# Buffers placed by the planner, a second tuning of its order, and eight planned weight chunks in an attention and two-layer feed-forward kernel

## The chip, the cores and the metric

The kernel runs on one core of one Trainium2 chip. The metric is device time in microseconds (us) of one execution, the median of several; lower is better. TensorE is PE in the rows, its weight loads PEld, VectorE DVE, ScalarE ACT, GpSimd POOL, and SyncE, which issues the DMAs, SP.

## What is computed

Per batch (2) and head (8), with 768 positions of width 64: queries and keys are hashed by the signs of six projections, a score counts only where the two hashes agree, and softmax times `v` follows. The result is the input (1536 tokens, width 512) of two feed-forward layers (512 to 2048 to 512), the first with a leaky rectifier, the second with `h*cos(h)`.

```python
mask = q_bucket[:, :, :, None] == k_bucket[:, :, None, :]
scores = scale * np.matmul(q, k.transpose(0, 1, 3, 2))
scores = np.where(mask, scores, -1000000000.0)
scores = scores - np.max(scores, axis=-1, keepdims=True)
attn = np.exp(scores)
attn = attn / (np.sum(attn, axis=-1, keepdims=True) + 1e-09)
x = np.matmul(attn, v)             # then, per layer:
h = x @ w_in
g = np.maximum(0.01 * h, h)        # layer 1; h * np.cos(h) in layer 2
x = g @ w_out
```

## The kernel before, in words

Every float32 operand of a matmul is split into a rounded part ("hi") and a remainder ("lo"), and three products stand for one.

**Attention.** 16 heads `n`, each in six key blocks `k`. Per head and block the items are: `mm` (2 matmuls, L284), a product whose row maximum `mr` (DVE, L290) gives the row's shift; `qk` (4 matmuls, L361 and L362), the scores; `ex` and `cv` (ACT), exponential and its rounded copy; `sub` (L383), the remainder; `pv` (4 matmuls) and `pw` (2 matmuls), both L396, values times hi and lo. Once a head: `bm` and `bw` (hash bits, L268 and L274), `rt` and `fl` (the maxima turned into a row), `pe`, `ev`, then `lc`, `rc`, `dw`, `rr`, `xm`, `xh`, `xl`, which divide by the sum and split the result into `XH` and `XL`. A head has 80 matmuls of 384 columns and one small one.

`sub` has two kinds, chosen by a letter per block in `LO`. With G, ACT writes the exponential to a tile `pf` in SBUF (L371), copies it rounded (L379), and POOL subtracts. With V, ACT computes the exponential twice, once rounded into `ph` (L368), once in place in PSUM (L376), and DVE subtracts from PSUM; the PSUM tile is taken until that is done. `mm`, `qk`, `bm`, `rt` and the sums of `v` share three PSUM tiles `st`.

**Feed-forward.** A step `s` is one block of 128 hidden columns `f` by 512 tokens: `mi` (12 matmuls, L655), `ga`, `gm`, `gh`, `gl` (activation and its split), `mo` (12 matmuls into four accumulators `y`, L700); after four blocks `ye` takes `y` away (L709, L711). Steps 0 to 11 use weight chunks 0 to 3 three times, steps 12 to 15 chunks 4 to 7. A chunk (1 MB of float64) is loaded (`wload`) and converted in seven pieces: `w0` (ACT, L580), `w1` and `w2` (DVE, L581 and L582), `w3` and `w4` (DVE, L583 and L573), `w5` (ACT, L584), `w6` (POOL, L577). `w3` and `w4` read two SBUF tensors.

**What sets the order.** `Plan.order` (L112) is a list scheduler: items with costs (`COST`), priorities (`KEY`, `FIX`, `CHUNK_KEY`) and dependencies are placed one after the other on five queues, and the order so found is the program order of each engine. It covers the attention, feed-forward steps 0 to 11 and the first `CHUNKS` = 6 chunks. Tiles come from pools that hand out their buffers in turn; the plan waits for the use that lies a ring's length back. From step 12 on `Moe.rest` (L745) writes the program: per step `Feed.tick` (L598) emits one stage of a chunk in work, and `Feed.until` (L617) emits the rest of a chunk at the step that needs it.

Of the kernel before, what the change touches and what calls it, by code (L numbers as in the profile page):

```python
# [28 lines left out]
TB = 512  # L29
NR = 4  # L30
LO = [{0: 'GGGGGG', 1: 'VGVGVV', 2: 'GVGGVG', 12: 'GGGVGV', 13: 'GVGGGG', 14: 'VGVVGV', 15: 'GGVGVV'}.get(n, "VGGGVG") for n in range(NH)]
CHUNKS = 6
# [3 lines left out]
    load=-118, hi=-28, d2=-23, d3=18, lo=-83, dl=-28, bm=-14.2, bw=-32, db2=-57, db1=-38, mm=-8.1, mr=-25,  # L36
    rt=-10, fl=82, neg=-50, dr=-48, de=-28, qk=0.8, ex=-6, cv=-29, sub=-21, pe=86, pv=4.7, pw=3.2, ev=-15,
    lc=10, rc=27, dw=-3, rr=-17, xm=56, xh=57, xl=20, vload=5, vh=25, vl=1, sv=-10.3, sh=101, sl=26, wload=58,
    w0=45, w1=73, w2=10, w3=62, w4=-37, w5=99, w6=-57, mi=-5, ga=-8, gm=-40, gh=80, gl=-47, mo=56, ye=2,
)  # L40
FIX = {
# [7 lines left out]
}  # L49
CHUNK_KEY = (95.9, 69.7, 115.6, 142.2, 66.7, 109.6, 173.8, 129.6)  # L50
# [43 lines left out]
class Plan:  # L94
# [4 lines left out]
    def __init__(self, rings, free):  # L99
        self.rings, self.free = rings, dict(free)  # L100
        self.items, self.index = [], {}

    def add(self, name, e, kind, key, fn, after=(), take=None, give=(), cost=None, moe=False):
        deps = [self.index[d] for d in after if d is not None and d in self.index]
        it = dict(name=name, e=e, kind=kind, key=(key, len(self.items)), fn=fn, deps=deps, take=take, give=list(give),
                  cost=COST[kind] if cost is None else cost, out=[], left=len(deps), moe=moe, before=[])
        for d in deps:
            d["out"].append(it)
        self.items.append(it)
        self.index[name] = it  # L110

    def order(self):  # L112
        free = {e: self.free.get(e, 0.0) for e in "PVAGQ"}
        ready = {e: [] for e in "PVAGQ"}
        taken = {r: [] for r in self.rings}
# [7 lines left out]
        def start(it):  # L123
            t = max(free[it["e"]], it["at"])
            r = it["take"]
            if r is not None:
                n = len(taken[r]) - self.rings[r]
                if n >= 0:
                    t = max(t, taken[r][n].get("end", 1e9))
            return t  # L130

        while len(done) < len(self.items):
# [26 lines left out]
            if it["take"] is not None:  # L159
                it["slot"] = {}  # L160
                taken[it["take"]].append(it["slot"])
                n = len(taken[it["take"]]) - 1 - self.rings[it["take"]]
                it["before"] = [taken[it["take"]][n]["by"]] if n >= 0 else []
            for g in it["give"]:
                self.index[g]["slot"].update(end=end + 0.06, by=it)
# [10 lines left out]
def attention(tc, ctx, plan, xp, dr_p, XH, XL, AT, VH, VL, YX, qkt, v, proj, cst, fd, more_raws, heads=NH):  # L176
# [3 lines left out]
    if True:  # L180
        pool = lambda n, b, **kw: ctx.enter_context(tc.tile_pool(name=n, bufs=b, **kw))
        con = pool("con", 1)
        raw_p = pool("raw", 2)
        vraw_p = pool("vraw", 1)
        phi_p = pool("phi", 3)
        plo_p = pool("plo", 3)
        pf_p = pool("pf", 2)
        sm_p = pool("sm", 3)
        sv_p = pool("svp", 1)
        st_ps = pool("st", 3, space=bass.MemoryType.PSUM)  # L190
        pv_ps = pool("pvp", 1, space=bass.MemoryType.PSUM)
# [9 lines left out]
        raw = {0: raw_p.tile([128, S], F32, name="raw")}  # L201
# [5 lines left out]
        E = [con.tile([128, S], F32R, name=f"e{i}") for i in range(2)]  # L207
        SV = [con.tile([128, 4, 128], F32R, name=f"sv{i}") for i in range(2)]
# [12 lines left out]
        neg = con.tile([1, S], F32, name="neg")  # L221
        G.memset(neg, -1.0)
        ident = con.tile([128, 128], F32R, name="ident")
# [21 lines left out]
        def load_qk(n):  # L245
            raw[n] = raw_p.tile([128, S], F32, name="raw")
# [33 lines left out]
        def max_mm(n, t):  # L280
            at = AT[n % NR]
            ps = st_ps.tile([128, 2, 512], F32, name="st")
# [31 lines left out]
        def load_v(g):  # L314
            vraw[g] = vraw_p.tile([128, C, 4, 64], F32, name="vraw")
# [12 lines left out]
        def sum_v(g):  # L328
            ps = st_ps.tile([128, 2, 512], F32, name="st")
# [25 lines left out]
        def qk(n, k):  # L355
            at = AT[n % NR]
            ps = st_ps.tile([128, 2, 512], F32, name="st")
# [43 lines left out]
        drs = {}  # L401
# [67 lines left out]
        for n in range(heads):  # L469
# [4 lines left out]
            if n:  # L474
                do("load", n, "Q", load_qk, n, take="raw" if n > 1 else None, after=[("load", n - 1), ("dr", n - 3)])
# [3 lines left out]
                do("lo", n, "G", lo, n, after=[("hi", n)], give=[("load", n)] if n > 1 else ())  # L479
# [379 lines left out]
```

## Time and profile before

| | us |
|---|---|
| median of 3 runs | 821.01 (820.14 to 821.43) |
| the profiled execution | 821.24 |
| its span, first to last instruction | 819.4 |
| PE busy in it | 786.8 |
| DVE, ACT, POOL busy | 479.5, 438.4, 432.4 |

The profile lists, for one execution, the busy time of each engine, and for each instruction what ended the engine's idle time before it. The program is in order on each engine, so a wait holds up all that stands behind it. Attention takes the span up to 264.8 us, where the first `mi` begins; feed-forward steps follow until the end. Busy shares are averages over stages; what a wait costs is read in its stage.

### The profile page before, as it was taken

What the parts mean: (1) busy time and instruction counts of PE and PEld (TensorE: products, weight loads), DVE (VectorE), ACT (ScalarE), POOL (GpSimd) and SP (SyncE); (2) the same over time, 40 slices, a digit from 0 to 9 for tenths busy, and PEclk for the clock granted to TensorE, in tenths of its full rate; (3) what the DMA queues carried; (4) which work ended last, traced back from release to release, by engine and by line L of the source; (5) the groups of instructions that cost most, each with busy time, mean ns of one, the idle gap of its engine ahead of it and who ended that gap; (6) DMA issues with size and microseconds to landing.
All of it is one profiled execution on the core that took longest, in us unless ns stands there. A gap on an engine that the chain in (4) does not pass through costs nothing. (4 is left out here: it accounts for less than half of the span.)

```text
span 819.4 us, 9862 instructions
## 1 busy us (share of the span) xinstructions
PE 786.8 (96%) x3648; PEld 667.8 (81%) x3648; DVE 479.5 (59%) x579; ACT 438.4 (53%) x630; POOL 432.4 (53%) x282
## 2 busy tenths in 40 slices
PE   6999999999899999779999999999999999999998
PEld 4899999989799788558888888887788888888886
DVE  7666666656777952337666356456747737743333
ACT  3777878867789424224333224355656555544442
POOL 8768887977778512223455334846623533532221
PEclk9999999999999999889999999999999999999999
DMA  6534534524531610112222112102202210000012
GB/s 177 149 84 111 147 91 102 138 64 109 167 110 57 215 68 1 52 52 90 70 98 103 52 52 102 52 4 100 102 1 66 89 52 1 0 1 2 0 52 103
DMA packets 24264, 63.19 MB, mean 77 GB/s; under 512 B 7684, under 2 KB 11428, under 8 KB 20120
## 3 DMA queue, kind: packets, MB, share of 16 engines
q1 hardware_dynamic: 24216, 62.56, 25.1%
q8 instruction: 29, 0.48, 0.2%
q14 instruction: 19, 0.16, 0.1%
HBM read 46.21 MB, written 3.19 MB: 60 GB/s over the span
## 5 line engine op out<-in xcount | busy, mean ns | idle before, releaser
L687 POOL TENSOR_TENSOR gl<-gf,gh 128x512 fp32r<-128x512 f32 x88 | 123.1, 1399 | 298.8 <-ACT gh L681 238.0
L700 PE MATMUL y<-gh,at 128*128 128x512 f32 x576 | 181.0, 395 | 1.6 <-ACT ys L709 1.6
L655 PE MATMUL h<-XH,at 128*128 128x512 f32 x576 | 143.9, 391 | 0.0
L383 POOL TENSOR_TENSOR pl<-pf,ph 128x768 fp32r<-128x768 f32 x62 | 116.3, 1884 | 40.1 <-ACT ph L379 33.3
L700 PEld LDWEIGHTS y<-gh,at 128*128 128x128 f32 x576 | 107.6, 187 | 28.1 <-ACT ys L709 2.0
L655 PEld LDWEIGHTS h<-XH,at 128*128 128x128 f32 x576 | 108.0, 188 | 24.9 <-POOL at L577 0.5
L290 DVE TENSOR_REDUCE mx<-st 128x1 fp32r<-128x768 f32 x96 | 90.9, 956 | 43.4 <-PE st L284 41.4
L700 PE MATMUL y<-gl,at 128*128 128x512 f32 x288 | 113.6, 395 | 0.7 <-POOL gl L687 0.7
L662 ACT ACTIVATE gf<-h 128x512 f32<-128x512 f32 x48 | 28.7, 598 | 143.1 <-PE h L655 127.0
L672 DVE TENSOR_TENSOR gf<-h,gf 128x512 f32<-128x512 f32 x48 | 33.1, 690 | 108.7 <-ACT gf L662 108.6
L666 ACT ACTIVATE ki<-h 128x512 int32<-128x512 f32 x48 | 28.7, 598 | 107.1 <-PE h L655 107.1
L655 PE MATMUL h<-XL,at 128*128 128x512 f32 x288 | 77.0, 389 | 0.0
L667 DVE SCALAR_TENSOR_TENSOR gf<-ki,h 128x512 f32<-128x512 int32 x48 | 33.0, 687 | 72.9 <-ACT ki L666 66.9
L361 PE MATMUL st<-at 77*128 77x384 f32 x192 | 67.4, 351 | 3.8 <-DVE mx L290 2.3
L700 PEld LDWEIGHTS y<-gl,at 128*128 128x128 f32 x288 | 53.9, 187 | 14.3 <-POOL gl L687 1.1
L362 PE MATMUL st<-at 128*128 128x384 f32 x192 | 65.2, 340 | 0.0
L577 POOL TENSOR_TENSOR at<-wsc,at 128x1024 fp32r<-128x1024 f32 x24 | 60.3, 2512 | 7.1 <-ACT at L584 7.1
L655 PE MATMUL h<-XH,wx 128*128 128x512 f32 x192 | 52.6, 417 | 11.2 <-ACT wx L584 10.5
L655 PEld LDWEIGHTS h<-XL,at 128*128 128x128 f32 x288 | 54.1, 188 | 11.4
L681 ACT ACTIVATE gh<-gf 128x512 fp32r<-128x512 f32 x96 | 59.8, 623 | 4.0 <-DVE gf L672 2.3
L371 ACT ACTIVATE pf<-st 128x768 f32<-128x768 f32 x62 | 50.1, 808 | 19.3 <-PE st L362 17.6
L676 DVE SCALAR_TENSOR_TENSOR gf<-gf,h 128x512 f32<-128x512 f32 x48 | 32.9, 685 | 46.2 <-ACT gf L675 46.2
(95 smaller groups left out, 1467.1 us busy)
## 6 DMA issues: line engine op xcount, KB each, us to landing
wrvh<-in_w_dram SPq DMA_DIRECT2D x16, 1024.0 KB
wrvl<-in_w_dram SPq DMA_DIRECT2D x16, 1024.0 KB
at<-at SPq DMA_DIRECT2D x63, 192.0 KB
raw<-in_qk_dram SPq DMA_DIRECT2D x15, 384.0 KB
vraw<-in_v_dram SPq DMA_DIRECT2D x4, 768.0 KB
yx<-dr SPq DMA_DIRECT2D x16, 192.0 KB
out_dram<-ys SPq DMA_DIRECT2D x6, 256.0 KB
out_dram<-yx SPq DMA_DIRECT2D x6, 256.0 KB
```

Source lines behind the costliest of these rows:

```text
L290: V.reduce_max(mx[n][:, t:t + 1], mps.pop((n, t))[:, :, 0:HS], axis=AX.XY)
L361: T.matmul(o, at[0:R76 + 1, 2, kc], at[0:R76 + 1, 0, COL[h]], start=True, stop=False)
L362: T.matmul(o, at[:, 3, kc], at[:, 1, COL[h]], start=False, stop=True)
L371: A.activation(pf[n, k], sps.pop((n, k)), AF.Exp, scale=SCALE)
L383: (V if LO[n][k] == "V" else G).tensor_tensor(halves(plo[n, k]), pf.pop((n, k)), halves(f32(phi[n, k])), op=ALU.subtract)
L577: G.tensor_tensor(lf, sc, f32(hf), op=ALU.subtract)
L655: self.tc.nc.tensor.matmul(ps, w[:, 0, k], x[:, k, cols], start=(j == 0), stop=(j == 3 * KT - 1))
L667: nc.vector.scalar_tensor_tensor(g, ki, -TWOPI, ps, op0=ALU.mult, op1=ALU.add)
L672: nc.vector.tensor_tensor(g, ps, g, op=ALU.max)
L681: self.tc.nc.scalar.activation(gh, self.gs[s], AF.Copy)
L687: (nc.vector if s < GLV else nc.gpsimd).tensor_tensor(gl, g, f32(gh), op=ALU.subtract)
L700: self.tc.nc.tensor.matmul(y, w[:, 1, e], x, start=(j == 0 and i == 0), stop=(j == GRP - 1 and i == 2))
```

## The change

`Plan` keeps for each ring the time at which each of its buffers comes free and gives an item the one that is free first; `plan.tile` hands the tile out by that place, and the pools are gone. 131 of the 229 times that `st` is taken, the buffer is not the next in turn; `phi` and `plo` also leave the turn, the other rings keep it. `LO`, `KEY`, `FIX`, `CHUNK_KEY` and six costs have new numbers: `w3` and `w4` from 0.95 to 1.15, `w5` 0.93 to 1.06, `w6` 2.37 to 2.4, `fl` 0.45 to 0.55, `ga` 0.63 to 0.6. By `LO`, 53 of the 96 `sub` are on DVE instead of 34; in heads 3 to 10 it is four of six instead of two. `CHUNKS` is 8. Tiles of a few bytes are allocated behind the large ones, so that large tiles start at multiples of 64 bytes.

```diff
-LO = [{0: 'GGGGGG', 1: 'VGVGVV', 2: 'GVGGVG', 12: 'GGGVGV', 13: 'GVGGGG', 14: 'VGVVGV', 15: 'GGVGVV'}.get(n, "VGGGVG") for n in range(NH)]
-CHUNKS = 6
+LO = [{0: 'GGGVGG', 1: 'VGGGVG', 2: 'GGVGVG', 11: 'GGGVGV', 12: 'GGVVGV', 13: 'GVGGGG', 14: 'VGVVVV', 15: 'VGVVVV'}.get(n, "VGVGVV") for n in range(NH)]
+CHUNKS = 8
-CHUNK_KEY = (95.9, 69.7, 115.6, 142.2, 66.7, 109.6, 173.8, 129.6)
+CHUNK_KEY = (132.0, 106.0, 116.9, 111.2, 249.3, 102.4, 235.2, 115.5)
...
+    def tile(self, ring):
+        return self.tiles[ring][self.place]
...
-            r = it["take"]
-            if r is not None:
-                n = len(taken[r]) - self.rings[r]
-                if n >= 0:
-                    t = max(t, taken[r][n].get("end", 1e9))
+            if it["take"] is not None:
+                t = max(t, min(end for end, _ in places[it["take"]]))
...
+                ring = places[it["take"]]
+                j = it["place"] = min(range(len(ring)), key=lambda j: ring[j][0])
+                it["before"] = [ring[j][1]] if ring[j][1] else []
+                ring[j] = (1e9, None)
             for g in it["give"]:
-                self.index[g]["slot"].update(end=end + 0.06, by=it)
+                g = self.index[g]
+                places[g["take"]][g["place"]] = (end + 0.06, it)
...
-            ps = st_ps.tile([128, 2, 512], F32, name="st")
+            ps = plan.tile("st")
...
-        neg = con.tile([1, S], F32, name="neg")
+        neg = con.tile([C, 128], F32, name="neg")
...
-            do("wload", c, "Q", wload, c, key=key - 8, after=[("pw", 11, C - 1), ("wload", c - 1), ("w4", c - 2)])
+            do("wload", c, "Q", wload, c, key=key - 8, after=[("pw", 11 if c < 6 else NH - 1, C - 1), ("wload", c - 1), ("w4", c - (2 if c < 6 else 4))])
...
-        ps = self.h[s] = self.h_ps.tile([128, TB], F32, name="h")
+        ps = self.h[s] = self.HP[s % 4]
...
-        sc_p = ctx.enter_context(tc.tile_pool(name="wscp", bufs=2))
+        sc_p = ctx.enter_context(tc.tile_pool(name="wscp", bufs=1))
+        sums = xp.tile([128, 64], F32, name="sums")
```

Three places on DVE show how the order moves. In the order of the change a name carries the number of its buffer, and its lines are those of the changed kernel: L299 is `mr`, L392 `sub`, L283 `bw`, L419 `rc`, L681 `gm`, L695 `gl`, L717 `ye`, and L589, L590, L591, L581 are `w1` to `w4`.

First, between steps 5 and 9 of the first layer. Before, from the sixth `gm` on:

```order
L687 TENSOR_TENSOR gl<-gf,gh 128x512
L672 TENSOR_TENSOR gf<-h,gf 128x512 x2
L687 TENSOR_TENSOR gl<-gf,gh 128x512
L672 TENSOR_TENSOR gf<-h,gf 128x512
L711 TENSOR_SCALAR ys_2902<-y_2976 128x512
L711 TENSOR_SCALAR ys_2904<-y_2978 128x512
L687 TENSOR_TENSOR gl<-gf,gh 128x512
```

Now, where `wsc_77` with `wrvh_2309` is chunk 6 and `wsc_78` with `wrvl_2310` chunk 7:

```order
L589 TENSOR_SCALAR wsc_77<-wsc_77 128x1024
L681 TENSOR_TENSOR gf_2327<-h_2341,gf_2327 128x512
L590 TENSOR_SCALAR wsc_77<-wsc_77 128x1024
L589 TENSOR_SCALAR wsc_78<-wsc_78 128x1024
L681 TENSOR_TENSOR gf_2326<-h_2338,gf_2326 128x512
L590 TENSOR_SCALAR wsc_78<-wsc_78 128x1024
L591 SCALAR_TENSOR_TENSOR wsc_78<-wrvl_2310,wsc_78 128x1024
L581 SCALAR_TENSOR_TENSOR wsc_78<-wrvl_2310,wsc_78 128x1024
L591 SCALAR_TENSOR_TENSOR wsc_77<-wrvh_2309,wsc_77 128x1024
L581 SCALAR_TENSOR_TENSOR wsc_77<-wrvh_2309,wsc_77 128x1024
L717 TENSOR_SCALAR ys_2347<-y_2343 128x512
L717 TENSOR_SCALAR ys_2349<-y_2345 128x512
```

The eight DVE pieces of chunks 6 and 7 now stand ahead of the `ye` of step 3; before, they stood behind the `gm` of steps 13 and 14.

Second, chunks 0 and 1 among heads 12 to 14. Before:

```order
L383 TENSOR_TENSOR pl<-st,ph 128x768
L581 TENSOR_SCALAR wsc<-wsc 128x1024
L582 TENSOR_SCALAR wsc<-wsc 128x1024
L274 TENSOR_SCALAR at_70<-st,cs 44x768
L583 SCALAR_TENSOR_TENSOR wsc<-wrvh_2332,wsc 128x1024
L573 SCALAR_TENSOR_TENSOR wsc<-wrvh_2332,wsc 128x1024
L290 TENSOR_REDUCE mx<-st 128x1 x2
```

Now:

```order
L589 TENSOR_SCALAR wsc_77<-wsc_77 128x1024
L283 TENSOR_SCALAR at_71<-st_109,cs 44x768
L392 TENSOR_TENSOR plo_93<-st_110,phi_90 128x768
L590 TENSOR_SCALAR wsc_77<-wsc_77 128x1024
L392 TENSOR_TENSOR plo_92<-st_108,phi_89 128x768
L299 TENSOR_REDUCE mx_107<-st_110 128x1
L299 TENSOR_REDUCE mx_107<-st_108 128x1
L589 TENSOR_SCALAR wsc_78<-wsc_78 128x1024
L590 TENSOR_SCALAR wsc_78<-wsc_78 128x1024
L299 TENSOR_REDUCE mx_107<-st_108 128x1
L591 SCALAR_TENSOR_TENSOR wsc_78<-wrvl_1887,wsc_78 128x1024
L392 TENSOR_TENSOR plo_92<-st_109,phi_88 128x768
```

`w3` and `w4` of chunk 0 no longer stand between `bw` of head 15 and the `mr` of head 14; they come after the last `mr` of head 15, and those of chunk 1 stand singly.

Third, the end of attention, from the last `sub` of head 14. Before:

```order
L581 TENSOR_SCALAR wsc<-wsc 128x1024
L582 TENSOR_SCALAR wsc<-wsc 128x1024
L583 SCALAR_TENSOR_TENSOR wsc<-wrvh_2332,wsc 128x1024
L383 TENSOR_TENSOR pl<-st,ph 128x768
L573 SCALAR_TENSOR_TENSOR wsc<-wrvh_2332,wsc 128x1024
L383 TENSOR_TENSOR pl<-st,ph 128x768
L411 RECIPROCAL rc<-lc 128x6
L383 TENSOR_TENSOR pl<-st,ph 128x768
```

Now:

```order
L590 TENSOR_SCALAR wsc_77<-wsc_77 128x1024
L591 SCALAR_TENSOR_TENSOR wsc_77<-wrvh_1886,wsc_77 128x1024
L581 SCALAR_TENSOR_TENSOR wsc_77<-wrvh_1886,wsc_77 128x1024
L392 TENSOR_TENSOR plo_92<-st_109,phi_90 128x768
L392 TENSOR_TENSOR plo_91<-st_110,phi_89 128x768
L589 TENSOR_SCALAR wsc_78<-wsc_78 128x1024
L590 TENSOR_SCALAR wsc_78<-wsc_78 128x1024
L392 TENSOR_TENSOR plo_92<-st_108,phi_90 128x768
L419 RECIPROCAL sums<-sums 128x6
L591 SCALAR_TENSOR_TENSOR wsc_78<-wrvl_1887,wsc_78 128x1024
L392 TENSOR_TENSOR plo_93<-st_109,phi_88 128x768
L392 TENSOR_TENSOR plo_91<-st_110,phi_89 128x768
```

Head 15 has five `sub` on DVE instead of three, and seven pieces of chunks 2 and 3 among them instead of four.

## Rows read from the trace of the kernel before

**Rows 1.** The profile's first part: busy us, share of the span, instructions.

```profile
PE 786.8 (96%) x3648; PEld 667.8 (81%) x3648; DVE 479.5 (59%) x579; ACT 438.4 (53%) x630; POOL 432.4 (53%) x282
```

**Rows 2.** Windows of PE, steps 12 to 15: us, PE busy (x), granted clock, DMA, GB/s.

```profile
323.10:328.64 5.54, 5.54 (x26) 1.00 0.00 0
328.64:361.43 32.79, 21.55 (x74) 0.79 0.19 64
```

**Rows 3.** Timeline of PE, steps 14 and 15: start, us, engine line op [idle <-releaser].

```profile
339.06 2.07 PE L655 MATMUL h<-XH,wx 128*128 128x512 f32 x4 [4.71 <-ACT wx L584]
...
353.38 2.07 PE L655 MATMUL h<-XH,wx 128*128 128x512 f32 x4 [5.79 <-ACT wx L584]
```

**Rows 4.** Timeline of DVE, 307 to 338 us: start, us, then as in rows 3.

```profile
307.90 0.69 DVE L711 TENSOR_SCALAR ys<-y 128x512 f32<-128x512 f32 x1 [7.75 <-PE y L700]
...
332.88 1.79 DVE L581 TENSOR_SCALAR wsc<-wsc 128x1024 f32<-128x1024 f32 x1
334.70 0.69 DVE L582 TENSOR_SCALAR wsc<-wsc 128x1024 int32<-128x1024 int32 x1
335.43 1.23 DVE L583 SCALAR_TENSOR_TENSOR wsc<-wrvh,wsc 128x1024 int32<-128x1024 int32 x1
336.69 1.22 DVE L573 SCALAR_TENSOR_TENSOR wsc<-wrvh,wsc 128x1024 int32<-128x1024 int32 x1
```

**Rows 5.** Windows: us, PE, PEld, DVE, ACT, POOL busy (x), granted clock, DMA, GB/s.

```profile
163.95:170.42 6.47, 4.72 (x18) 4.21 (x18) 2.93 (x6) 2.22 (x3) 4.34 (x3) 0.74 0.20 40
215.10:232.50 17.40, 14.18 (x69) 13.33 (x69) 16.24 (x18) 11.79 (x15) 8.08 (x4) 0.90 0.61 187
262.20:264.90 2.70, 2.17 (x13) 1.77 (x12) 2.59 (x5) 2.70 (x4) 1.88 (x1) 1.00 0.47 112
```

**Rows 6.** The same view, the even stretch of attention.

```profile
100.00:160.00 60.00, 60.00 (x342) 57.76 (x341) 38.30 (x50) 47.64 (x63) 51.53 (x29) 1.00 0.44 108
```

**Rows 7.** Timelines of PE, ACT and POOL at 163 to 167 us.

```profile
166.21 0.71 PE L284 MATMUL st<-at 76*128 76x384 f32 x2 [1.75 <-ACT pf L371]
...
165.35 0.81 ACT L371 ACTIVATE pf<-st 128x768 f32<-128x768 f32 x1 [0.83 <-POOL pl L383]
...
163.48 3.60 POOL L383 TENSOR_TENSOR pl<-pf,ph 128x768 fp32r<-128x768 f32 x2
```

**Rows 8.** Timelines of PE and DVE at 220 to 225 us.

```profile
224.15 0.44 PE L361 MATMUL st<-at 77*128 77x384 f32 x1 [2.30 <-DVE mx L290]
...
220.36 2.75 DVE L573 SCALAR_TENSOR_TENSOR wsc<-wrvh,wsc 128x1024 int32<-128x1024 int32 x1
```

**Rows 9.** Groups by line and form, 20 to 210 us: busy us, mean ns.

```profile
L290 DVE TENSOR_REDUCE mx<-st 128x1 fp32r<-128x768 f32 x77 | 73.5, 958 | 37.4 <-PE st L284 35.5
L383 DVE TENSOR_TENSOR pl<-st,ph 128x768 fp32r<-128x768 f32 x24 | 23.0, 958 | 11.6 <-ACT st L376 10.6 <-POOL pl L383 0.4 <-POOL XL L432 0.3
L274 DVE TENSOR_SCALAR at<-st,cs 44x768 fp32r<-44x768 f32 x13 | 14.1, 1086 | 12.7 <-PE st L268 6.0 <-POOL yx L423 2.6 <-issue 1.7
...
L383 POOL TENSOR_TENSOR pl<-pf,ph 128x768 fp32r<-128x768 f32 x50 | 91.8, 1843 | 33.5 <-ACT ph L379 27.9 <-DMA raw<-in_qk_dram 1.9 <-PE st L284 1.7
L432 POOL TENSOR_TENSOR XL<-yx,XH 128x768 fp32r<-128x768 f32 x5 | 9.2, 1841 | 0.0
...
L376 ACT ACTIVATE st<-st 128x768 f32<-128x768 f32 x24 | 19.3, 806 | 0.0
```

**Rows 10.** The same groups, whole span: `gl` on DVE.

```profile
L687 DVE TENSOR_TENSOR gl<-gf,gh 128x512 fp32r<-128x512 f32 x8 | 11.6, 1465 | 1.0 <-ACT gh L681 1.0
```

**Rows 11.** Timeline of DVE and POOL at 270 to 313 us.

```profile
270.85 0.68 DVE L687 TENSOR_TENSOR gl<-gf,gh 128x512 fp32r<-128x512 f32 x1
...
312.57 1.29 POOL L687 TENSOR_TENSOR gl<-gf,gh 128x512 fp32r<-128x512 f32 x1 [16.40 <-ACT gh L681]
```

**Rows 12.** Timelines of POOL and ACT at the start.

```profile
11.89 1.82 POOL L254 TENSOR_TENSOR at<-raw,at 128x768 fp32r<-128x768 f32 x1
...
7.51 0.84 ACT L250 ACTIVATE at<-raw 128x768 fp32r<-128x768 f32 x1 [0.95 <-DMA raw<-in_qk_dram]
```

More of the change, by code (lines that the diff above doesn't have):

```diff
@@ L105, in add @@
         it = dict(name=name, e=e, kind=kind, key=(key, len(self.items)), fn=fn, deps=deps, take=take, give=list(give),
-                  cost=COST[kind] if cost is None else cost, out=[], left=len(deps), moe=moe, before=[])
+                  cost=COST[kind] if cost is None else cost, out=[], left=len(deps), moe=moe, before=[], place=0)
         for d in deps:
@@ L114, in order @@
         ready = {e: [] for e in "PVAGQ"}
-        taken = {r: [] for r in self.rings}
+        places = {r: [(0.0, None)] * k for r, k in self.rings.items()}
         wire = port = 0.0
@@ L173, in order, with attention @@
         return done
-def attention(tc, ctx, plan, xp, dr_p, XH, XL, AT, VH, VL, YX, qkt, v, proj, cst, fd, more_raws, heads=NH):
+def attention(tc, ctx, plan, sums, dr_p, XH, XL, AT, VH, VL, YX, qkt, v, proj, cst, fd, more_raws, heads=NH):
     nc = tc.nc
@@ L182, in attention, with ring @@
         con = pool("con", 1)
[L183 to L191, printed above, removed]
+        psum = pool("psum", 1, space=bass.MemoryType.PSUM)
+        def ring(name, shape, dtype=F32, p=con):
+            plan.tiles[name] = [p.tile(shape, dtype, name=f"{name}{i}") for i in range(plan.rings[name])]
+        ring("raw", [128, S])
+        ring("vraw", [128, C, 4, 64])
+        ring("phi", [128, S], F32R)
+        ring("plo", [128, S], F32R)
+        ring("pf", [128, S])
+        E = [con.tile([128, S], F32R, name=f"e{i}") for i in range(2)]
+        SV = [con.tile([128, 4, 128], F32R, name=f"sv{i}") for i in range(2)]
+        ring("svt", [128, 2, 2, 64], F32R)
+        ring("mt", [C, 2, 128])
+        ident = con.tile([128, 128], F32R, name="ident")
+        ring("mx", [128, C], F32R)
+        ring("st", [128, 2, 512], p=psum)
+        ring("pv", [128, 2, 512], p=psum)
+        DR = [dr_p.tile([1, S], F32, name=f"dr{i}") for i in range(4)]
         OS = [YX[:, i * S:(i + 1) * S] for i in range(2)]
         RR, XX = (YX[:, i * S:(i + 1) * S] for i in (2, 3))
-        LC, RC = (xp.tile([128, 4, C], F32, name=n) for n in ("lc", "rc"))
+        LC, RC = (sums[:, i * 4 * C:(i + 1) * 4 * C].rearrange("p (a b) -> p a b", b=C) for i in range(2))
         cs = con.tile([128, 130], F32, name="cs")
@@ L200, in attention @@
         Q.dma_start(pj[64:128], proj)
-        raw = {0: raw_p.tile([128, S], F32, name="raw")}
+        raw = {0: plan.tiles["raw"][0]}
         COL = [slice(h * HS, (h + 1) * HS) for h in range(2)]
@@ L281, in max_mm @@
             at = AT[n % NR]
-            ps = st_ps.tile([128, 2, 512], F32, name="st")
+            ps = plan.tile("st")
             for h in range(2):
@@ L328, in sum_v @@
         def sum_v(g):
[L329 removed]
+            ps = plan.tile("st")
             vs = (VH[g % 2], VL[g % 2])
@@ L474, in attention @@
             if n:
-                do("load", n, "Q", load_qk, n, take="raw" if n > 1 else None, after=[("load", n - 1), ("dr", n - 3)])
+                do("load", n, "Q", load_qk, n, take="raw", after=[("hi0", 0), ("load", n - 1), ("dr", n - 3)])
                 do("hi", n, "A", hi, n, after=[("load", n)] + old)
@@ L678, in high @@
     def high(self, s):
-        gh = self.g_p.tile([128, TB], F32R, name="gh")
-        gl = self.g_p.tile([128, TB], F32R, name="gl")
+        gh, gl = (t[s % (LAG + 1)] for t in (self.GH, self.GL))
         self.tc.nc.scalar.activation(gh, self.gs[s], AF.Copy)
@@ L694, in mm_out @@
         j = f % GRP
-        if j == 0:
-            self.ys[l, b] = [self.y_ps.tile([128, TB], F32, name=f"y{e}") for e in range(KT)]
         for e in range(KT):
-            y = self.ys[l, b][e]
+            y = self.YP[e]
             for i, (w, x) in enumerate(((wh, gh), (wl, gh), (wh, gl))):
@@ L808, in emit @@
                 seen.add(id(it))
+                plan.place = it["place"]
                 it["fn"]()
```

118 lines of the change are left out of this document (55 added, 63 removed), and 15 rows, old and new, of the table FIX.

## The prediction

> **What bounds the kernel now.** I read the busy times first. PE is busy 786.8 us, 96% of the span, and no other engine above 59% [rows 1], so the time falls only where PE waits or runs slowly. The next view is therefore PE stage by stage, in windows. The reader is to see three kinds of place. The dearest is steps 13 to 15 of the first layer: step 12 takes 5.54 us, and the next 32.79 us hold only three steps, at a granted clock of 0.79 [rows 2]. The timeline of PE names the releaser: steps 14 and 15 wait 4.71 and 5.79 us for the conversion of chunks 6 and 7 on ACT [rows 3]. Behind ACT stands DVE: chunk 6's four DVE pieces follow each other only from 332.88 us on [rows 4], because the unplanned feeder gives out one stage per step. The other two kinds lie in attention, one stretch at 164 us and one at 215 to 232 us, with the granted clock at 0.74 and 0.90 [rows 5]. The even stretch between them is full: 342 matmuls in 60.00 us, 0.175 us each [rows 6]. That pace is the yardstick for the two bad stretches.
>
> **The change, part by part.** All sums are against the profiled execution of 821.24 us, 0.2 above the median of 821.01.
>
> *Chunks 6 and 7 are planned.* Three steps at 5.54 us would take 16.6 us; they take 32.79 [rows 2]. If both chunks are ready, 16.2 us go, the stretch at half clock behind each wait included. No instruction is added: the same seven pieces a chunk move ahead, past `gm` and `ye` on DVE and past some `ga` on ACT, and their two loads go ahead of and behind the last `rr` on SP. What covers them? A chunk's DVE pieces cost 0.69, 0.69, 1.23 and 1.22 [rows 4] (the first took 1.79 there, beside a POOL subtraction; I set it as the second), 3.8 us, so 7.7 us for two. They now stand around `gm` of steps 7 and 8 and ahead of `ye` of step 3, where DVE sat idle for 7.75 us [rows 4], while PE has eight `mi` in a row. They fit, barely. If that cover fails, `ye` comes late and the next `mo`, which wants its accumulators, waits. Upwards the price is bounded by stretching: one such piece took 2.75 us beside POOL [rows 8] instead of 1.22, 1.5 more, and two of the last four stand beside POOL's `w6` of the other chunk, 3.1 us. A wait of 1.75 us cost 3.3 in all (next term), so up to 5.8. I take nothing, since POOL has a gap of 16.40 us there [rows 11]; the term lies between 10.4 and 16.2.
>
> *Two of six `sub` per head leave POOL for DVE in heads 3 to 10.* At 164 us PE waits 1.75 us for a `st` tile that ACT empties, ACT waits for a `pf` tile, and POOL is two `sub` behind [rows 7]. The stretch holds 18 matmuls, worth 3.2 us, and lasts 6.47 [rows 5]: 3.3 us. With two `sub` of 1.84 us less [rows 9] POOL is relieved of 3.7 us a head, more than that wait. I take 3.3, down to 0 if DVE makes the same wait.
>
> DVE pays: per head six `mr` at 0.958, two `sub` at 0.958, `bw` 1.09 [rows 9] and about 0.7 of small ones, 9.5 us, become 11.4, against 80 matmuls, 14.0 us, on PE. There is room, but less, and each moved `sub` holds its `st` tile longer, by the second exponential of 0.81 and the `sub` of 0.96 [rows 9]. Giving out the tile that is free first works against that. Between nothing and one stall as at 164 us in each of eight heads (26 us) I take a loss of 1 us, near nothing, since the even stretch runs full with DVE at 38.30 of 60.00 us [rows 6].
>
> *Chunks 0 and 1 are spread out.* In the window from 215.10 to 232.50 us 69 matmuls, worth 12.1 us, take 17.40: 5.3 us [rows 5]. PE waits for an `mr` [rows 8] behind `w3` and `w4`, of which one took 2.75 us. In the new order, from the second `mr` of head 14 to the first of head 15, I count 14.1 us of DVE work by these durations and 78 matmuls, 13.7 us, on PE. So DVE is still the later one by 0.4 us, and two stretched pieces add up to 3.1. I take 2 us of loss left, so 3.3 won, between 1.9 and 5.3.
>
> *The end of attention is denser on DVE.* From the third-last `sub` of head 14 on, DVE has eight `sub` (7.7), seven pieces (6.4) and a reciprocal, 14.3 us; PE has 76 matmuls, 13.3 us, from the `pw` behind the first of them. Less that first `sub`, plus the last two `pw` (0.7), DVE is late by 0.7 us, with three stretched pieces by 5.3. Today this place costs 0.4: 13 matmuls in 2.70 us [rows 5]. I take 2 us more than today; between 0.4 won and 4.9 lost.
>
> *Edits that I cost at nothing.* The three `neg` transfers now go out ahead of head 1's load, but its rounding is done at 8.4 us while POOL begins the remainder only at 11.89 [rows 12]: 3.5 us of cover. If it failed, head 1's maxima would come later by the excess. The places of large tiles change no duration that I can find: POOL subtracts 128x768 in 1.843 us where its tiles were off the multiple of 64 bytes, and in 1.841 where they were on it [rows 9]. Feed-forward tiles keep their turn.
>
> The sum: 16.2 + 3.3 - 1 + 3.3 - 2 = 19.8 us; 821.24 - 19.8 = 801.4, and 0.2 less for the median: **801 us**. With the terms at their better ends it is 796, and with chunk 6 and 7 stretched and both attention terms at their worse ends about 813.
>
> **The rivals.**
>
> *A, attention loses nearly all its waits: 791.* The busy row of PE says that the even stretch is full, but its weight loads are busy 57.76 of 60.00 us [rows 6], 3.7% less. Over 245 us of attention that would be 9 us more to win, of which I grant half, 5, beyond the 796. The Trainium skill, "Perfetto Trace Analysis", section Identifying the Most-Contended Engine, holds that matmul busy time is a bad measure of the distance to the roofline and that the weight loads' share is a good one; by it, the room is there. Against it: an order can only win it if PE was waiting in pieces too short to be shown.
>
> *B, attention gives back what it wins: 805 to 811.* The heavier DVE makes as many waits as it removes, and only the 16.2 us stay, or part of them. For it: DVE is ahead of PE by nothing at two places, worked out above. Against it: POOL's backlog is gone for certain.
>
> *C, the moved pieces become the next wait: 808 to 815.* Chunks 6 and 7 push `ye` of step 3 beyond its idle time, at the price above, or their loads come late.
>
> *D, slower: 833.* Every `sub` that moves to DVE is stretched by POOL as `gl` on DVE is: 1.465 us on the mean [rows 10] where one alone took 0.68 [rows 11], a factor of 2.15. Then four `sub` a head cost 4.4 us more, 15.8 against 14.0 on PE, and ten heads fall behind by 1.8 us each. With the half clock behind every wait, which made 3.3 us of 1.75 [rows 5, 7], that is 33 us lost, about 833. It decides from the point where a `sub` on DVE takes over 1.6 us. Against it: the 24 such `sub` took 0.958 us on the mean [rows 9] while POOL was busy 51.53 of 60.00 us [rows 6]. The Trainium skill, "GPSIMD Engine Reference", section 1, Specifications, says that POOL shares its SBUF interfaces with VectorE and contends with instructions that read two SBUF inputs. By it, `gl` and the last two DVE pieces of a chunk are stretched, and `sub`, which reads one operand from PSUM, is not; the rows agree.
>
> *E, the order changes and the time doesn't,* within 0.2% of 821, about what a measurement of this kernel can tell from no change. The chunks would have to be late for another reason, or attention to lose all that they win.
>
> **How the numbers follow.** Forecast 0.57, A 0.13, B 0.20, C 0.05, D 0.03, E 0.02. The range from 792 to 811 holds the forecast's own cases, nearly all of B, about half of A and of C. Faster by over 0.2% is all but D and E: 0.95; within 0.2% 0.02; slower 0.03. The time is that of the likeliest case.
>
> **What would show it.** Right: the windows of steps 13 to 15 each 5.5 us at clock 1.00, and no wait of `mi` for line `w5`; `w3` and `w4` of chunks 6 and 7 ahead of `ye`; no wait of ACT for POOL in heads 9 and 10; some waits of PE for DVE at the ends of heads 12 to 15. Wrong: PE at 100 to 160 us with fewer than 342 matmuls in 60 us; the first `mi` later than 262 us; a wait of `mo` for `ye` in step 4; `sub` on DVE well above 0.96 us.

## The result and the profile after

The change makes the kernel faster: 796.28 us median (795.25 to 798.52) against 821.22 (820.14 to 822.15), a ratio of 0.97 with a 95% interval of 0.9676 to 0.9724. The forecast was 801.0, 4.7 us above the result, and the parts differ by more than that. The profiled executions, on which the parts are read, have spans of 819.4 and 796.7 us.

The profile's first row and two windows, steps 12 and 13 to 15 of the changed kernel (us, busy and count of PE, PEld, DVE, ACT, POOL, granted clock, DMA, GB/s), answer to [rows 1] and [rows 2]:

```profile
PE 774.5 (97%) x3648; PEld 666.6 (84%) x3648; DVE 475.3 (60%) x598; ACT 435.3 (55%) x630; POOL 409.1 (51%) x263
...
318.92:324.36 5.44, 5.44 (x26) 4.51 (x25) 1.73 (x3) 2.06 (x4) 2.57 (x2) 1.00 0.02 5
324.36:340.68 16.32, 16.32 (x74) 13.52 (x73) 5.71 (x7) 5.46 (x9) 2.26 (x2) 1.00 0.00 0
```

The three steps take 16.32 us instead of 32.79. But step 12, which waits for nothing in either kernel, has also become shorter, 5.44 against 5.54. The next views, windows of attention and of the even feed-forward, of the changed kernel and then of the kernel before:

```profile
100.00:160.00 60.00, 59.81 (x341) 57.74 (x340) 43.33 (x58) 47.69 (x64) 38.21 (x21) 1.00 0.43 107
160.00:170.00 10.00, 10.00 (x59) 9.71 (x58) 7.42 (x11) 6.72 (x10) 7.62 (x5) 1.00 0.37 80
210.00:250.00 40.00, 35.89 (x177) 33.01 (x178) 31.39 (x35) 27.88 (x36) 26.25 (x14) 0.91 0.38 126
250.00:262.00 12.00, 11.54 (x66) 11.08 (x65) 9.60 (x10) 11.97 (x17) 4.43 (x2) 1.00 0.39 141
...
400.00:500.00 100.00, 100.00 (x443) 82.79 (x442) 55.73 (x68) 35.72 (x53) 50.73 (x28) 1.00 0.21 74
```

```profile
160.00:170.00 10.00, 8.25 (x39) 7.71 (x38) 5.28 (x8) 5.92 (x8) 7.48 (x5) 0.83 0.40 90
210.00:250.00 40.00, 36.23 (x195) 34.58 (x194) 29.24 (x37) 30.97 (x40) 29.96 (x16) 0.96 0.44 137
250.00:262.00 12.00, 11.80 (x67) 11.28 (x66) 9.95 (x6) 11.25 (x16) 10.19 (x6) 1.00 0.06 17
...
400.00:500.00 100.00, 100.00 (x435) 81.22 (x434) 58.66 (x67) 34.55 (x50) 42.35 (x26) 1.00 0.21 76
```

Read the counts of matmuls behind PE's busy time. The stop at 164 us is gone (59 instead of 39). From 210 to 250 us there are fewer than before (177 against 195). And from 400 to 500 us PE is busy without a gap in both, at clock 1.00 in both, and yet does 443 matmuls instead of 435. One cut at the first `mi` separates the stages. Each stage is read from one profiled execution; each ratio is to runs of the kernel before taken beside, whose medians were 819.43 to 821.22 us:

| kernel | median, us | ratio to before (interval) | first `mi` | from there to the end | matmuls, 400 to 500 us |
|---|---|---|---|---|---|
| before | 821.22 | | 264.8 | 554.6 | 435 |
| the change | 796.28 | 0.97 (0.9676 to 0.9724) | 266.9 | 529.8 | 443 |
| a_padg | 803.07 | 0.9779 (0.976 to 0.9799) | 264.4 | 538.4 | 435 |
| a_all64 | 797.85 | 0.9705 (0.9681 to 0.9729) | 266.3 | 529.7 | 443 |
| b_padg | 812.65 | 0.9894 (0.9875 to 0.9912) | 262.8 | 548.0 | 442 |
| b_chunks8 | 807.76 | 0.9839 (0.9817 to 0.9862) | 262.5 | 544.7 | 435 |
| a_vload | 795.28 | 0.9697 (0.9675 to 0.9718) | 263.1 | 529.8 | 442 |
| a_w3 | 794.39 | 0.9687 (0.9665 to 0.9709) | 263.3 | 529.8 | 443 |
| a_both | 794.1 | 0.969 (0.9668 to 0.9712) | 262.4 | 529.8 | 443 |
| a_oldorder | 809.23 | 0.9851 (0.9824 to 0.9878) | 274.2 | 530.1 | 443 |
| a_g64 | 803.09 | 0.9806 (0.9771 to 0.984) | 266.3 | 538.9 | 435 |
| a_t64 | 805.2 | 0.9817 (0.9782 to 0.9853) | 267.1 | 537.7 | 436 |
| a_wx64 | 800.91 | 0.979 (0.9758 to 0.9822) | 260.8 | 534.3 | 440 |
| a_rot | 834.47 | 1.0184 (1.0149 to 1.022) | 302.9 | 531.4 | 443 |

So the feed-forward became 24.8 us shorter and attention, in these two executions, 2.1 us longer: three surprises against the prediction. 24.8 is 8.6 more than the 16.2 of the three steps; attention should have won 3.6; and the place where it was to win, chunks 0 and 1, is where it lost.

### The profile page after: what moved, and what is told of

Read it like the earlier page. It is cut to its first block, busy times and chain, and to the rows that moved or that the text cites. A ratio compares the mean times of both kernels' runs of the same rounds, so it can differ in the third digit from the quotient of the medians.

```text
span 796.7 us, 9934 instructions
## 1 busy us (share of the span) xinstructions
PE 774.5 (97%) x3648; PEld 666.6 (84%) x3648; DVE 475.3 (60%) x598; ACT 435.3 (55%) x630; POOL 409.1 (51%) x263
## 5 line engine op out<-in xcount | busy, mean ns | idle before, releaser
L695 POOL TENSOR_TENSOR gl<-gf,gh 128x512 fp32r<-128x512 f32 x88 | 134.8, 1532 | 264.2 <-ACT gh L689 200.5
L706 PE MATMUL y<-gh,at 128*128 128x512 f32 x576 | 177.7, 390 | 1.8 <-ACT ys L715 1.7
L664 PE MATMUL h<-XH,at 128*128 128x512 f32 x576 | 142.3, 389 | 0.0
L299 DVE TENSOR_REDUCE mx<-st 128x1 fp32r<-128x768 f32 x96 | 90.3, 953 | 37.7 <-PE st L293 35.9
L392 POOL TENSOR_TENSOR plo<-pf,phi 128x768 fp32r<-128x768 f32 x43 | 80.9, 1885 | 58.3 <-ACT phi L388 52.6
L681 DVE TENSOR_TENSOR gf<-h,gf 128x512 f32<-128x512 f32 x48 | 33.2, 691 | 107.4 <-ACT gf L671 107.3
L706 PE MATMUL y<-gh,wx 128*128 128x512 f32 x192 | 59.1, 389 | 0.0
L392 DVE TENSOR_TENSOR plo<-st,phi 128x768 fp32r<-128x768 f32 x53 | 50.3, 952 | 11.7 <-ACT st L385 10.3
```

What stands on the lines that cost most here:

```text
L664: self.tc.nc.tensor.matmul(ps, w[:, 0, k], x[:, k, cols], start=(j == 0), stop=(j == 3 * KT - 1))
L681: nc.vector.tensor_tensor(g, ps, g, op=ALU.max)
L695: (nc.vector if s < GLV else nc.gpsimd).tensor_tensor(gl, g, f32(gh), op=ALU.subtract)
L706: self.tc.nc.tensor.matmul(y, w[:, 1, e], x, start=(j == 0 and i == 0), stop=(j == GRP - 1 and i == 2))
```

## The experiments

Names that begin with a_ are edits of the changed kernel, with b_ of the kernel before.

**Where the large tiles stand: the pace of PE.** Theory 1 started from the allocation: before, x and the `at` weights lie at 128 modulo 256 bytes, and g, `ys` and `wx` at 64; in the changed kernel all agree. These tiles stood at multiples of 64 bytes before, too: what the change altered is how far they stand apart.

```diff
 # a_padg and, at the same place, b_padg (Moe.begin)
+        ctx.enter_context(self.tc.tile_pool(name="pad", bufs=1)).tile([128, 16], F32, name="pad")
 # a_all64
-        sums = xp.tile([128, 64], F32, name="sums")
+        sums = xp.tile([128, 80], F32, name="sums")
```

a_padg: 

> The changed kernel with 64 unused bytes ahead of the feed-forward tiles, so that g, ys and the four wx tiles lie 64 bytes off a multiple of 128, as in the kernel before, while x and the other weights stay on one; attention is untouched. Theory 1 (a matmul is slower where its weights and its moving operand stand at different places within 128 bytes): three mo matmuls go from 0.68 back to 0.70 us, some 435 instead of 443 matmuls in 100 us, and the time goes from 796.3 to 803 to 806 us. Theory 2 (the pace comes from tiles that are allotted once instead of by pools in turn, or from the engine's clock): no change, 795 to 798 us.

a_all64: 

> The changed kernel with every large tile moved by the same 64 bytes, x and all weights among them. Theory 1 in its form by difference: weights and moving operand keep the same distance, so no change, 795 to 798 us. Theory 1 in its form by place (any operand off a multiple of 128 bytes costs): at least the loss of the previous run, 803 to 806 us or more, attention's matmuls included.

b_padg: 

> The kernel before with 64 bytes ahead of the feed-forward tiles, which brings g, ys and wx onto a multiple of 128 bytes; its pools, its order and its six planned chunks stay. Theory 1: 7 to 9 us faster, 812 to 814 us, with attention unchanged and three mo matmuls at 0.68 us. Theory 2: no change, 820 to 822 us.

All three came out as theory 1 in its form by difference said: 803.07, 797.85 and 812.65 us, 435, 443 and 442 matmuls in 100 us. Pools, order and clock (1.00 in that window everywhere) have no part in it. b_padg won 6.6 us behind the first `mi` and not 8.6: its three steps 13 to 15 still wait, and took 34.15 us instead of 32.79, which is 1.4 of the missing 2.0. Three more runs asked which tiles it is:

```diff
 # a_g64: pads of 64 bytes ahead of g_p and of y_p; a_t64: ahead of t_p and of g_p
+        pd(1, 16)
         g_p = pool("g", 1)
 # a_wx64: a pad of 64 bytes ahead of ep
+        ctx.enter_context(tc.tile_pool(name="pad", bufs=1)).tile([128, 16], F32, name="pad")
         ep = ctx.enter_context(tc.tile_pool(name="ep", bufs=1, reuse_waits="tile"))
```

a_g64: 

> The changed kernel with only the eight tiles gh and gl (the moving operands of mo) 64 bytes off a multiple of 128; gf, ki, ys, wx, x and all weights stay on one. Theory 1a (PE's own two operands at different places within 128 bytes): mo is slow, some 435 matmuls in 100 us while the weights are at tiles, 802 to 804 us. Theory 1b (the other engines' accesses to gf disturb PE): no change, 795 to 798 us.

a_t64: 

> The changed kernel with only gf and ki, which PE never reads, 64 bytes off a multiple of 128. Theory 1a: no change, 443 matmuls in 100 us, 795 to 798 us. Theory 1b: some 435 to 439 in 100 us, 799 to 804 us.

a_wx64: 

> The changed kernel with only the four wx tiles (the weights of two chunks in eight) 64 bytes off a multiple of 128. Theory 1a: both mi and mo are slow in the quarter of the steps that use them, 0.1 us a step for 24 steps, 798 to 799.5 us, and the steps with at weights stay at 5.44 us. Theory 1b: no change, 795 to 798 us, and no step above 5.44 us.

a_g64 came out as 1a said, though its second pad moved `ys` and `wx` by 128 bytes as well. a_t64 did not: 805.2, where 1a expected no change. The totals alone would now speak for 1b, by which accesses to the tile `gf`, which PE never reads, slow PE. The groups of PE by operands decide it. First a_t64, then a_wx64, 400 to 780 us (line, tile out<-in, form, count, busy us, mean ns, idle before):

```profile
L711 PE MATMUL y<-gh,at 128*128 128x512 f32 x416 | 130.6, 395 | 1.6 <-ACT ys L720 1.6
L669 PE MATMUL h<-XH,at 128*128 128x512 f32 x416 | 103.5, 391 | 0.0
...
L711 PE MATMUL y<-gh,wx 128*128 128x512 f32 x132 | 40.7, 390 | 0.0
L669 PE MATMUL h<-XH,wx 128*128 128x512 f32 x128 | 32.4, 394 | 0.0
```

```profile
L706 PE MATMUL y<-gh,at 128*128 128x512 f32 x416 | 128.7, 390 | 1.7 <-ACT ys L715 1.7
L664 PE MATMUL h<-XH,at 128*128 128x512 f32 x408 | 100.9, 389 | 0.0
...
L706 PE MATMUL y<-gh,wx 128*128 128x512 f32 x131 | 41.3, 395 | 0.0
L664 PE MATMUL h<-XH,wx 128*128 128x512 f32 x144 | 36.5, 396 | 0.0
```

In a_t64 the second pad stands behind the first, so gh, gl, `ys` and `wx` moved by 128 bytes, which I had taken for harmless. Where gh meets `wx`, both moved alike, the matmul takes 390 ns, though `gf` is 64 bytes off there too; where one operand moved by 128 and the other did not, 394 and 395. In a_wx64 only the pairs with `wx` are slow, and a step with `at` weights keeps its 5.44 us; behind the first `mi` it lost 4.5 us (534.3 against 529.8), more than the 2.4 expected: both products of a step with `wx` are slow there, which makes 0.19 us a step instead of 0.1. Its own time, 796.85 to 804.82, scatters too much to tell. The two lines of a step with `at` weights in the same view of the kernel before, and then of the changed kernel:

```profile
L700 PE MATMUL y<-gh,at 128*128 128x512 f32 x416 | 130.8, 395 | 1.6 <-ACT ys L709 1.6
L655 PE MATMUL h<-XH,at 128*128 128x512 f32 x416 | 103.8, 391 | 0.0
```

```profile
L706 PE MATMUL y<-gh,at 128*128 128x512 f32 x416 | 128.4, 390 | 1.8 <-ACT ys L715 1.7
L664 PE MATMUL h<-XH,at 128*128 128x512 f32 x416 | 102.7, 389 | 0.0
```

Eight kernels together, by how far the weights and the moving operand of a matmul stand apart modulo 256 bytes (mean ns of that view, XL and gl within 2 of XH and gh):

| kernel | XH on `at` | gh on `at` | XH on `wx` | gh on `wx` |
|---|---|---|---|---|
| before | 0: 391 | 64: 395 | 64: 394 | 0: 391 |
| b_padg | 0: 389 | 0: 390 | 0: 389 | 0: 389 |
| the change | 0: 389 | 0: 390 | 0: 389 | 0: 389 |
| a_all64 | 0: 389 | 0: 390 | 0: 389 | 0: 389 |
| a_padg | 0: 393 | 64: 394 | 64: 394 | 0: 391 |
| a_g64 | 0: 393 | 64: 393 | 128: 395 | 64: 396 |
| a_t64 | 0: 391 | 128: 395 | 128: 394 | 0: 390 |
| a_wx64 | 0: 389 | 0: 390 | 64: 396 | 64: 395 |

A pair that stands 64 or 128 apart takes 393 to 396 ns, and a kernel without any such pair has 389 or 390 everywhere. So 1a holds with 256 in the place of 128. A longer period isn't needed: in b_padg gh on `at` and XH on `wx` stand an odd multiple of 256 bytes apart, in the change an even one, and both kernels have 389 and 390. What stays open is XH on `at`, a pair that agrees, in kernels where the other pair of the same step doesn't: 393 in a_padg and a_g64, 391 in before and a_t64. `gf` alone, without the 128 bytes behind it, was not tried.

Attention bounds the rule. There `ph` and `vh` stood 32 bytes apart in the kernel before, and `phi` and `vh` agree in the change, yet a matmul of 384 columns did not become faster (before, then the change, 100 to 160 us):

```profile
L396 PE MATMUL pv<-ph,vh 128*128 128x384 f32 x50 | 12.8, 336 | 0.0
```

```profile
L405 PE MATMUL pv<-phi,vh 128*128 128x384 f32 x50 | 12.9, 339 | 0.0
```

The loss is shown for 512 columns and distances of 64 and 128 bytes, and not beyond.

**The old tables with eight chunks.**

```diff
-CHUNKS = 6
+CHUNKS = 8
...
-after=[("pw", 11, C - 1), ("wload", c - 1), ("w4", c - 2)])
+after=[("pw", 11 if c < 6 else NH - 1, C - 1), ("wload", c - 1), ("w4", c - (2 if c < 6 else 4))])
```

b_chunks8: 

> The kernel before with eight planned chunks instead of six, its tables of numbers and its pools unchanged. If the 16.2 us of steps 13 to 15 are the chunks' alone: no wait of mi for w5, the first mi still at 264 to 266 us, and 803 to 806 us. If the old numbers cannot place two more chunks without making ye or gm late: waits of PE for DVE in steps 2 to 9, and 806 to 815 us.

807.76: the second case. The waits for `w5` are gone, but 554.6 - 544.7 = 9.9 us are won and not 16.2. The timeline of PE and the window around it show what took their place:

```profile
285.69 0.80 PE L700 MATMUL y<-gl,at 128*128 128x512 f32 x1 [3.16 <-DVE gl L687]
...
280.00:290.00 10.00, 6.84 (x21) 5.13 (x20) 9.93 (x6) 4.42 (x7) 6.95 (x3) 0.74 0.28 105
```

DVE is full (9.93 of 10.00), `gl` comes late behind chunk pieces, and the clock falls behind the wait. The bill that rival C drew up is real, at `gl` and not at `ye`, in an order that was not made for eight chunks. The new order has no such wait; a_oldorder below, with the old tables and the new buffer rule, has none either, so the tables alone don't make it.

**Attention: piece `w3` of chunk 0.** In the changed kernel PE stops at 240 and at 242 us and then runs at a granted clock of 0.50 up to 248 (timelines of PE, DVE and POOL):

```profile
240.28 0.44 PE L370 MATMUL st<-at 77*128 77x384 f32 x1 [0.94 <-ACT pf L380]
242.44 0.69 PE L370 MATMUL st<-at 77*128 77x384 f32 x1 [1.18 <-DVE plo L392]
243.89 0.84 PE L397 MATMUL pv<-e,sv 128*128 128x384 f32 x2
...
238.16 3.36 DVE L591 SCALAR_TENSOR_TENSOR wsc<-wrvh,wsc 128x1024 int32<-128x1024 int32 x1
242.31 1.97 DVE L581 SCALAR_TENSOR_TENSOR wsc<-wrvh,wsc 128x1024 int32<-128x1024 int32 x1
...
236.83 1.84 POOL L392 TENSOR_TENSOR plo<-pf,phi 128x768 fp32r<-128x768 f32 x1
238.63 1.81 POOL L439 TENSOR_TENSOR XL<-yx,XH 128x768 fp32r<-128x768 f32 x1
241.24 1.96 POOL L392 TENSOR_TENSOR plo<-pf,phi 128x768 fp32r<-128x768 f32 x1 [0.80 <-POOL XL L439]
```

`w3` (L591) ends at 241.52, which is 1.08 us behind the end of POOL's XL (240.44); `w4` ends at 244.28, 1.08 behind POOL's next one (243.20). A piece of 1.2 us alone stands still until POOL's instruction is done, here through two of them.

```diff
 # a_w3 (a_both has this line and that of a_vload)
         work = plan.order()
+        work.insert(work.index(plan.index[('w2', 0)]) + 1, work.pop(work.index(plan.index[('w3', 0)])))
```

a_w3: 

> The changed kernel with one instruction moved on DVE: piece w3 of chunk 0 from behind the maxima of head 15 to straight behind w2 of that chunk, where POOL is idle. Theory 4 (a piece that reads two SBUF operands is stretched by POOL, and this one, at 3.36 us, causes the stop and the half clock at 238 to 248 us): w3 takes 1.2 to 1.4 us at the new place, the stop at 240 to 248 us goes, 210 to 250 us holds 190 to 200 matmuls instead of 179, 793 to 795 us. Rival (DVE simply has too much work there, wherever the piece stands): PE waits for mx or at at 222 to 226 us instead, no gain, 796 to 798 us.

At its new place `w3` takes 1.23 us (the lines are DVE's, of a_w3), the stop of 1.18 us is gone, and 210 to 250 us holds 193 matmuls:

```profile
220.25 1.23 DVE L591 SCALAR_TENSOR_TENSOR wsc<-wrvh,wsc 128x1024 int32<-128x1024 int32 x1
...
224.71 2.34 DVE L590 TENSOR_SCALAR wsc<-wsc 128x1024 int32<-128x1024 int32 x1
```

Theory 4's size is not shown: `w2` of chunk 1, one operand, now meets POOL and takes 2.34 instead of 0.69, and the median of 794.39 has an interval that overlaps that of the change. A comparison that no edit made says more. In the change, a_padg, a_all64, a_g64 and a_t64, whose attention is the same program, `w3` took 3.35 to 3.38 us, and the first `mi` came at 264.4 to 267.1; in a_wx64, again the same program, it took 1.58, and the first `mi` came at 260.8. In a_vload it also took 1.58. These are the lines of a_vload, DVE and POOL:

```profile
238.32 1.58 DVE L591 SCALAR_TENSOR_TENSOR wsc<-wrvh,wsc 128x1024 int32<-128x1024 int32 x1
...
236.99 1.83 POOL L392 TENSOR_TENSOR plo<-pf,phi 128x768 fp32r<-128x768 f32 x1
238.78 2.81 POOL L439 TENSOR_TENSOR XL<-yx,XH 128x768 fp32r<-128x768 f32 x1
```

Again the piece ends 1.08 us behind POOL's first instruction (238.82), and now POOL's second one is the one that waits, 2.81 instead of 1.81. In these two executions the stop of PE for that `sub` is absent, and in the change, a_padg and a_all64 it is 1.2 to 1.4 us: the stop went along with which of the two engines came first between POOL's instructions. What the two cost in all stays open.

**Attention: the start.**

```diff
         work = plan.order()
+        work.insert(work.index(plan.index[('neg', 3)]) + 1, work.pop(work.index(plan.index[('vload', 0)])))
```

a_vload: 

> The changed kernel with one transfer moved on SP: the first load of v goes out ahead of the two transfers of head 0 that stand before it, as in the kernel before. Theory 3 (the later start of attention comes from v landing late: PE waits 1.6 us for POOL's remainder of v): that wait falls below 0.5 us, the first mm of head 1 goes from 23.8 to about 22 us, the first mi comes 1.5 to 2.5 us earlier, 794 to 795 us. Rival (head 0's transfers are late instead, and head 0's chain is the one that counts): first mm of head 1 and total unchanged or up to 1 us later, 796 to 798 us.

a_both: 

> Both moves together. Theories 3 and 4: they add up, 4 to 6 us, 790 to 793 us. If either is wrong: the better of the two alone.

This doesn't decide on theory 3, since v did not come early. In a_vload its load went out earlier, and ACT began with v later (first the change, then a_vload; SP and ACT):

```profile
8.90 0.63 SPq L325 DMA_DIRECT2D vraw<-in_v_dram  x1
15.41 1.58 ACT L331 ACTIVATE vh<-vraw 128x768 fp32r<-128x768 f32 x2 [4.04 <-DMA vraw<-in_v_dram]
```

```profile
7.15 0.64 SPq L325 DMA_DIRECT2D vraw<-in_v_dram  x1
15.92 1.58 ACT L331 ACTIVATE vh<-vraw 128x768 fp32r<-128x768 f32 x2 [4.56 <-DMA vraw<-in_v_dram]
```

In the kernel before the load went out at 5.95 and ACT began at 12.30. So PE's wait for v stayed (first line the change, second a_vload), and head 1's first `mm` came at 24.46 instead of 23.84 us:

```profile
19.97 0.47 PE L342 MATMUL st<-vl,ones 128*65 128x256 f32 x1 [1.65 <-POOL vl L335]
```

```profile
20.48 0.48 PE L342 MATMUL st<-vl,ones 128*65 128x256 f32 x1 [2.15 <-POOL vl L335]
```

In seven executions with the load in its place (the change, a_w3 and the five that move tiles), ACT begins with v at 14.27 to 15.50 us, and head 1's first `mm` comes at 22.16 to 24.02, the later the later v came, but for one. That is in favour of theory 3. Against it stands a_both: ACT began with v at 14.96, and head 1 came at 24.34 all the same. So theory 3 is neither shown nor refuted, and why the load lands late is open.

What a_vload won (first `mi` at 263.1) lies at 230 to 250 us, where `w3` took 1.58; it was not aimed at. a_both, 794.1 us, adds nothing to a_w3. It has the lowest median of all, but its interval overlaps that of the change, so no version here is shown to beat it.

**The rule for buffers and the tables of the order.**

```diff
 # a_rot (Plan.order)
-                t = max(t, min(end for end, _ in places[it["take"]]))
+                ring = places[it["take"]]
+                t = max(t, ring[turn[it["take"]] % len(ring)][0])
...
-                j = it["place"] = min(range(len(ring)), key=lambda j: ring[j][0])
+                j = it["place"] = turn[it["take"]] % len(ring)
+                turn[it["take"]] += 1
 # a_oldorder: LO, KEY, FIX, CHUNK_KEY and COST of the kernel before, CHUNKS = 8
```

a_oldorder: 

> The changed kernel with the planner's tables of the kernel before (keys, fixed keys, chunk keys, costs, and who subtracts), eight chunks, aligned tiles and the free-first choice of buffers kept. If the new tables are worth what I forecast (164 us, chunks 0 and 1): attention longer by 3 to 4 us than in the changed kernel, first mi at 268 to 271 us, 799 to 803 us. If, as the traces say, the new tables made attention 2 to 3 us longer and serve chunks 6 and 7 alone: first mi at 262 to 265 us, one wait of PE for gl near 3 us, 796 to 800 us.

a_rot: 

> The changed kernel with its planner made to give out each ring's buffers in turn, as the pools of the kernel before did; tables, eight chunks and aligned tiles stay. If the free-first choice itself saves the waits (164 us): that wait returns and the first mi comes 3 to 10 us later, 799 to 806 us. If the choice is worth nothing by itself and the tables carry the gain: first mi at 263 to 268 us, 795 to 798 us.

Both lie outside what I expected. The new tables with buffers given out in turn bring the first `mi` to 302.9 us instead of 266.9, and the kernel to 834.47, slower than before. The old tables with the free-first rule bring it to 274.2, where in turn (b_chunks8) it was 262.5. Neither is good alone. That the tables fit the rule under which they were made is the reading nearest to these four numbers; the 36 us and 12 us don't add up to a worth of either. In a_oldorder PE waits three times each for `mx` and for POOL's `plo` (2.0 and 1.9 us); eight chunks cost it no wait behind the first `mi`, 530.1 us.

## Why the prediction was right, and where it was not

The sum of 19.8 us was 16.2 for the boundary and 3.6 for attention. The traces show 16.2, 8.6 that was forecast as nothing, and -2.1: 22.7, the difference of the two spans. The medians differ by 24.9: the profiled execution of the change, 798.52 us, was 2.2 longer than its median. Its first `mi` came at 266.9; the same program of attention has it at 260.8 to 267.1 in six executions, that of before at 264.8 and 262.8 in two. So attention won nothing that shows.

That 801 came so near is luck in part. a_padg is the change without the faster pace, which is what the prediction added up, and takes 803.07 us. Attention gave back what it won, as rival B described with 805 to 811, and a term that was put at nothing made up for it. Rival A's room was not touched: in the even stretch the weight loads are busy 57.74 us now and were 57.76. The worse end of "about 813" adds up to 811 by its own terms.

- *Chunks 6 and 7, 16.2 us: right in place and size.* 24.8 less the 8.6 that a_padg gives back (538.4 against 529.8) is 16.2. That the cover "fits, barely" was apt: b_chunks8 shows the stop when it doesn't fit.
- *"The places of large tiles change no duration that I can find": the step that failed, mis-sized by 8.6 us.* I looked for it in POOL's groups alone [rows 9]. The same view of PE, in the feed-forward, had it: before, a matmul of gh on `at` took 395 ns and one of XH on `at` 391, equal in shape. The runs showed that the place counts in PE, where the two operands of a matmul stand apart. Over 96 steps the 8.6 us are 0.09 a step.
- *The stall at 164 us, 3.3: gone as forecast, its size at the upper end, its cause not separated.* The wait is gone, 59 matmuls instead of 39, 20 of 0.175 us, so 3.5. But b_padg and b_chunks8, with that wait, hold 48 and 49 there at clock 1.00: the half clock behind it comes in some executions only, and without it 1.8 are won. And a_oldorder, with two `sub` per head on DVE, and a_rot, with four but the old rule, don't have that wait either: the moved `sub` aren't shown to be what removed it.
- *Four `sub` per head on DVE, -1: near.* 341 matmuls instead of 342 in the even stretch; `sub` took 0.952 us on the mean, so rival D's stretching, as argued, leaves it alone. The free-first rule, which works against longer holds of `st`, I named in a sentence and gave no price; in a_rot, without it, the even stretch holds 322 matmuls and the first `mi` comes 36 us later.
- *Chunks 0 and 1 spread out, +3.3: wrong.* 177 to 188 matmuls from 210 to 250 us in five executions (203 in the sixth) against 195 and 198 in two of before: in five nothing won, up to 3.7 us lost. I allowed for stretched pieces at 1.5 us each; `w3` lost 2.1, and stands where PE waits for the `sub` behind it.
- *The end of attention, -2.* 66 against 67 matmuls from 250 to 262 us: the end costs next to nothing.
- *The start, 0: wrong by 2.4 us in the execution profiled.* Head 1's first `mm` came at 23.84 against 21.41, and 1.65 of it is PE's wait for v. The prediction looked at the load of head 1, whose cover held (rounded at 10.82, before POOL at 11.31), and not at that of v, which goes out 2.95 us later than before. That this is the cause is not shown.

Two signs that I had named for a wrong forecast appeared: a first `mi` later than 262 us, and, by one matmul, fewer than 342 in the even stretch. The forecast came out 4.7 us too high because one term of 8.6 was overlooked, while chunks 0 and 1 and the start had been forecast too well.

## What to carry to other kernels

Group PE's matmuls by their operands and compare mean durations of equal shapes: 4 ns in 390 is invisible in a busy share of 100% and was worth 8.6 us here. Give the weights and the moving operand of a wide matmul (512 columns here) the same place modulo 256 bytes, and don't let small tiles shift the large ones. Place DVE work with SBUF operands where POOL is idle, and judge an order only under the buffer rule for which it was made.

## What the runs showed of the hardware

- A matmul of 128x512 whose weights and moving operand stand 64 or 128 bytes apart modulo 256 takes 393 to 396 ns instead of 389 or 390, and 435 instead of 443 run in 100 us. Moving everything by 64 bytes costs nothing (a_all64), and with 384 columns 32 bytes apart cost nothing (336 ns against 339). PE's busy share and clock don't mark such a loss, 100.00 of 100.00 us at 1.00 from 400 to 500 us both before and in the change; the count does, and the weight loads' time, 81.22 against 82.79 us.
- Beside POOL, the pieces `w3` and `w4` of the rows above end 1.08 us behind the end of a POOL instruction: 3.36 us instead of 1.23 where POOL ran two in a row, 1.58 where POOL's next one waited for the piece, 2.81 instead of 1.81. `w2`, which reads one SBUF operand, took 2.34 instead of 0.69 as well, while `sub`, with one of two operands in PSUM, kept its 0.952. The Trainium skill, "SBUF — State Buffer", section Terms, says that VectorE and GpSimd share a port pair as an exclusive lock that is held for a whole instruction and blocks the loser entirely. The trace agrees for the pieces, and shows besides that the turn between two POOL instructions goes sometimes to the one engine and sometimes to the other.
- The half clock behind a wait isn't certain: 0.83 at 160 to 170 us in one execution of before, 1.00 in b_padg's, with the same program up to there and a wait of 1.71 instead of 1.75 us:

```profile
160.00:170.00 10.00, 8.29 (x48) 7.87 (x47) 5.23 (x8) 6.19 (x9) 8.19 (x5) 1.00 0.40 91
```
